# Decode attention over a key cache: one early load split by rows into five transfers

## The chip, the cores and the metric

The kernel runs on one core of a Trainium2 chip. The metric is the device time of one execution in microseconds (us). The time before is 1305.89 us, the median of 2 runs (1305.44 to 1306.35).

## The reference

One decode step of a transformer block for a batch of 2: layer norm, attention over a cache of 8192 keys and values for each of 16 heads of 256, then a bilinear feed-forward block. All is float32. The key and value caches are 268 MB each, so nearly all of the work is to read them once.

```python
B, Sq, D = 2, 1, 448
H, Sk, Dh = 16, 8192, 256
...
q = (layernorm(x) @ wq).reshape(B, Sq, H, Dh).transpose(0, 2, 1, 3)
scores = einsum("bhqd,bhkd->bhqk", q, k_cache) * (Dh ** -0.5)
p = softmax(scores, axis=-1)
o = einsum("bhqk,bhkd->bhqd", p, v_cache)
h = x + o.transpose(0, 2, 1, 3).reshape(B, Sq, H * Dh) @ wo
...
g, u = layernorm(h) @ w_gate, layernorm(h) @ w_up
h2 = h + (g * u) @ w_down
```

## The kernel before

A "query" is one pair of head and batch item; there are NQ = 32. Query i has 8192 keys, laid out so that each of the 128 partitions holds NJ = 64 keys in a row: `keys(cache, i, lo, hi)` is the view of keys lo to hi of every partition, 1 KB per key and partition. A load of all 64 keys is 8.4 MB in 128 rows of 64 KB; a load of 16 keys is 2.1 MB in 128 rows of 16 KB.

The keys go to `k_sb`, which has room for 112 keys per partition: query 0, 2, 4 ... sit at keys 0 to 63 (`k_base` 0), query 1, 3, 5 ... at 48 to 111. The 16 places in the middle are shared, so the keys of query n+1 can be loaded once the first part of query n (its HC = 16 keys in the shared places) has been scored. The values go to `v_sb`, one buffer of 64, reloaded when TensorE has used it up. The weights of the next heads go to `w_sb`.

All these loads are issued by SP, in the order of the program, on one queue. An order waits on SP until its buffer is free, and the loads behind it wait with it. The order is: the weights of the first heads (`d_w0`), query 0's keys in three pieces (`FIRST`: keys 48 to 64, 0 to 16, 16 to 48), query 1's keys, query 0's values, query 2's keys, weights, query 1's values, and so on. The last queries' values are cut into smaller pieces (`LATE`), and the weights of the feed-forward block come last, into `k_sb`. ACT's queue has only the load of x at the start and half of the output at the end.

VectorE does the scores: a product of the keys with the query, written over the keys (`tensor_mul`), and a sum over the 256 entries (`tensor_reduce`). `score_parts` cuts a query in two parts (16 and 48 keys), and for the queries in `FINE` (0, 30 and 31) in four of 16. For query 0 these are keys 48 to 64, 0 to 16, 16 to 32 and 32 to 48. TensorE and ScalarE do the softmax's sums and exponentials and the mix of the values.

Waits are worked out by the class `Orders`. Each order names the regions that it reads and writes; a load writes a region of `k` given in elements of a partition's row, and gets a semaphore of its own name, which counts to 16. An order that touches a region waits for every load whose region overlaps it. A region of `k` says nothing of partitions.

Every instruction but the DMA issues is recorded by one helper, so the profile shows line 206 for nearly all of them and line 154 for the DMA issues; they are told apart by their tiles.

Of the kernel before, what the change touches and what calls it, by code (L numbers as in the profile page):

```python
# [10 lines left out]
B, D, H, SK, DH, F = 2, 448, 16, 8192, 256, 1792  # L11
EPS = 1e-5
P = 128
# [38 lines left out]
EARLY = NQ - len(LATE)  # L52
LOOP = EARLY
DOWN = (4, 4, 4, 2)
FINE = (0, NQ - 2, NQ - 1)


# [136 lines left out]
def decode_block(nc, x, k_cache, v_cache, w, wg, wu, wd, out):  # L194
    o = Orders(nc)

    def sb(name, *shape):
        return nc.alloc_sbuf_tensor(name, list(shape), F32)[:]
# [25 lines left out]
    k_sb = sb("k_sb", P, 2 * NJ - OVER, DH)  # L224
# [4 lines left out]
    def keys(cache, i, lo, hi):  # L229
        h, b = divmod(i, B)  # L230
        return cache[b, h].rearrange("(p j) d -> p j d", p=P)[:, lo:hi, :]

    def load_keys(name, cache, i, lo, hi, buf, at, event=None):
        o.load(
            "SP", name, buffers[buf][:, at : at + hi - lo, :], keys(cache, i, lo, hi),
            writes=[(buf, at * DH, (at + hi - lo) * DH)], event=event,
        )

    def k_base(i):
        return i % 2 * (NJ - OVER)  # L240

    def load_k(i, lo=0, hi=NJ):
        load_keys(f"d_k_{i}_{lo}", k_cache, i, lo, hi, "k", k_base(i) + lo)
# [15 lines left out]

    load_w("d_w0", 0, 0, WQ)  # L260
    for lo, hi in FIRST:
        load_k(0, lo, hi)

    ident = sb("ident", P, P)
    put("POOL", "memset", ident, 0.0, w=["ident"])
# [82 lines left out]
    for k in range(2):  # L348
        for b in range(B):
            for c in range(DC):  # L350
                at = c * 2 * DH + (k * DH if c < DC - 1 else 0)
# [47 lines left out]
    def score_parts(i):  # L399
        at = [(k - 1) % (NJ // HC) * HC if i % 2 == 0 else k * HC for k in range(NJ // HC)]  # L400
        if i in FINE:
            return [(lo, lo + HC) for lo in at]
# [141 lines left out]
    for n in range(NQ + 1):  # L544
        hp, at = divmod(n, 2 * B)
# [53 lines left out]
    for name, t, src in (("wg", wg_t, wg), ("wu", wu_t, wu)):  # L599
        for k, half in enumerate(halves):  # L600
            o.load("SP", f"d_{name}_{k}", t[:, half], src[:, half],
                   writes=[("k", places[name] + half.start, places[name] + half.stop)])
    at = 0
    for n in DOWN:
        o.load("SP", f"d_wd_{at}", wd_t[:, at * D : (at + n) * D], wd[:, at * D : (at + n) * D],
               writes=[("k", at * D, (at + n) * D)])
# [181 lines left out]
```

## Time and profile before

| what | value |
|---|---|
| time, median of 2 runs | 1305.89 us (1305.44 to 1306.35) |
| profiled execution, its own time | 1305.48 us |
| its span | 1304.1 us |
| VectorE busy | 1130.9 us (87%) |
| TensorE matmul busy | 489.5 us (38%) |
| ScalarE busy | 62.7 us (5%) |
| read from memory | 561.19 MB, 430 GB/s over the span |

The span is the time from the first to the last instruction that the profiler saw; the profiled execution took 1.4 us more than that. The page's slices give the busy share in tenths of each engine in 40 equal pieces of the span; the row DMA is the mean over the core's 16 DMA engines. The chain that ended last is followed back from the last instruction, at each step to what released it. In an issue row the last number is the median time from the issue to the landing. A packet in the DMA view is a row of a transfer, or a completion of 4 bytes, which counts one of a semaphore's 16 steps.

### The profile page before, as it was taken

The page shows a single profiled execution, that of the slowest core. Times are in us where ns is not written, and L with a number is a line of the kernel's source. Part 1 is how long each engine was busy: PE and PEld are TensorE (multiplying, and loading weights), DVE is VectorE, ACT ScalarE, POOL GpSimd, SP SyncE. Part 2 cuts the span into 40 slices and gives each one's busy share as a digit, 9 for nine tenths or more (in the row PEclk, how much of TensorE's full clock was granted, in tenths as well). Part 3 has the DMA queues.
Part 4 walks back from the last instruction along what each step waited for, and adds up shares of the span by engine and source line. Part 5 has one row for each costly group of instructions (what it writes and reads, how often), then busy time and mean ns, then how long its engine had stood idle before and what let it go on. Part 6 is the DMA issues. An engine that isn't in the chain of part 4 may idle for free.

```text
span 1304.1 us, 6966 instructions
## 1 busy us (share of the span) xinstructions
PE 489.5 (38%) x3004; PEld 170.0 (13%) x3004; DVE 1130.9 (87%) x279; ACT 62.7 (5%) x184; POOL 1.3 (0%) x8
## 2 busy tenths in 40 slices
PE   3036332263431634305333243433423334233277
PEld 2012110020100201102101011100101011011013
DVE  7997998878988789987889878889788898899981
ACT  1000000000000000000000000000000000000000
POOL 0000000000000000000000000000000000000000
PEclk8567766686665766658676576665767666566678
DMA  9999999999999999999999999999999999999998
GB/s 413 432 428 447 422 446 422 442 420 446 422 445 416 448 420 448 420 440 438 430 428 440 436 424 444 424 421 441 446 422 442 418 446 422 445 425 427 432 423 363
DMA packets 13136, 561.35 MB, mean 430 GB/s; under 512 B 1474, under 2 KB 1476, under 8 KB 2372
## 3 DMA queue, kind: packets, MB, share of 16 engines
q1 hardware_dynamic: 13112, 561.19, 99.7%
q8 instruction: 7, 0.11, 0.0%
q14 instruction: 5, 0.04, 0.0%
q10 hardware_dynamic: 12, 0.01, 0.0%
HBM read 561.19 MB, written 0.00 MB: 430 GB/s over the span
## 4 chain that ended last, share of the span: by engine, by line
DMA 73%; DVE 25%; PE 1%; issue 0%; ACT 0%; SPq 0%; POOL 0%; POOLq 0%; DVEq 0%
DMA k_sb<-in_A_k_cache_dram 68%; DVE k_sb L206 12%; DVE s L206 12%; DMA k_sb<-in_A_v_cache_dram 3%; DMA k_sb<-in_wd_dram 3%; DVE nm L206 0%; PE o_ps L206 0%; PE q_ps L206 0%; PE sm L206 0%; PE y_ps L206 0%; DVE xb L206 0%; DVE o_ps L206 0%; SPq L154 0%; ACT o_sb L206 0%; POOL ident L206 0%
## 5 line engine op out<-in xcount | busy, mean ns | idle before, releaser
L206 DVE TENSOR_TENSOR k_sb<-k_sb,q 128x4096 f32<-128x4096 f32 x70 | 556.4, 7949 | 133.6 <-DMA k_sb<-in_A_k_cache_dram 129.9
L206 DVE TENSOR_REDUCE s<-k_sb 128x16 f32<-128x4096 f32 x70 | 556.1, 7945 | 0.3
L206 PE MATMUL o_ps<-v_sb,p 128*2 128x512 f32 x2000 | 292.2, 746 | 397.5 <-PEq L161 374.6
L206 PEld LDWEIGHTS o_ps<-v_sb,p 128*2 128x2 f32 x2000 | 54.2, 97 | 606.8 <-issue 579.6
L206 PE MATMUL sm<-nm,row 1*128 1x1 f32 x64 | 16.8, 329 | 195.9 <-PEq L161 172.4
L206 PE MATMUL sm<-ident,m 128*1 128x128 f32 x32 | 10.6, 331 | 140.9 <-PEq L161 101.0
L206 PE MATMUL q_ps<-w_sb,xb 128*128 128x256 f32 (+1 forms) x172 | 59.2, 502 | 0.0
L206 ACT ACTIVATE o_sb<-o_ps 128x512 f32<-128x512 f32 x32 | 19.1, 597 | 689.2 <-PE o_ps L206 689.2
L206 PE MATMUL sm<-sel,o_sb 128*128 128x1 f32 x256 | 33.7, 253 | 25.7 <-PEq L161 22.1
L206 PEld LDWEIGHTS sm<-nm,row 1*128 1x128 f32 x64 | 14.8, 287 | 205.2 <-issue 180.3
L206 PE MATMUL acc_ps<-w_sb,oT 128*2 128x448 f32 x60 | 36.3, 743 | 12.4 <-PEq L161 11.6
L206 PEld LDWEIGHTS sm<-sel,o_sb 128*128 128x128 f32 x256 | 31.8, 195 | 56.1 <-issue 46.5
L206 PEld LDWEIGHTS q_ps<-w_sb,xb 128*128 128x128 f32 x172 | 33.6, 200 | 30.0 <-issue 27.6
L206 PE MATMUL sm<-lsum,ones 128*128 128x1 f32 x64 | 17.3, 339 | 26.0 <-PEq L161 22.3
L206 ACT ACTIVATE nb<-sm 128x1 f32<-128x1 f32 x32 | 5.5, 171 | 414.9 <-PE sm L206 414.9
L206 PEld LDWEIGHTS sm<-ident,m 128*1 128x1 f32 x32 | 2.6, 80 | 152.3 <-issue 109.3
L206 PEld LDWEIGHTS sm<-lsum,ones 128*128 128x128 f32 x64 | 15.4, 298 | 28.0 <-issue 23.9
L206 ACT ACTIVATE q<-q_ps,rstd 128x512 f32<-128x512 f32 (+1 forms) x18 | 11.5, 640 | 70.6 <-PE q_ps L206 70.6
L206 DVE TENSOR_REDUCE total<-o_ps 128x1 f32<-128x128 f32 x1 | 0.3, 292 | 15.7 <-PE o_ps L206 15.7
L206 ACT ACTIVATE p<-s,nb 128x64 f32<-128x64 f32 x32 | 11.2, 349 | 1.0
L206 PE MATMUL q_ps<-k_sb,xr 128*32 128x256 f32 (+1 forms) x128 | 10.3, 445 | 0.7 <-DVE xr L206 0.7
L206 ACT ACTIVATE oT<-sm,rl 128x2 f32<-128x2 f32 x32 | 8.4, 262 | 39.1 <-PE sm L206 39.1
(80 smaller groups left out, 78.3 us busy)
## 6 DMA issues: line engine op xcount, KB each, us to landing
v_sb<-in_A_v_cache_dram SPq DMA_DIRECT2D x4, 4096.0 KB, 30.6
w_sb<-in_w_dram SPq DMA_DIRECT2D x7, 1792.0 KB, 33.6
v_sb<-in_A_v_cache_dram SPq DMA_DIRECT2D x1, 7168.0 KB, 26.3
v_sb<-in_A_v_cache_dram SPq DMA_DIRECT2D x1, 6144.0 KB, 28.4
k_sb<-in_A_k_cache_dram SPq DMA_DIRECT2D x2, 2048.0 KB, 11.2
k_sb<-in_A_k_cache_dram SPq DMA_DIRECT2D x1, 4096.0 KB, 24.2
k_sb<-in_A_v_cache_dram SPq DMA_DIRECT2D x1, 4096.0 KB, 37.7
v_sb<-in_A_v_cache_dram SPq DMA_DIRECT2D x3, 1024.0 KB, 23.4
```

The lines of the kernel that those rows point to most:

```text
L206: o.put(engine, lambda: f(*args, **kw), r, w, mark, event)
```

## The change

The second of query 0's three loads, keys 0 to 16 of all 128 partitions, becomes five loads of the same keys: partitions 0 to 111, 112 to 119, 120 to 123, 124 and 125, and 126 and 127. They are issued by SP one after the other at the place of the old load, each with a semaphore of its own. Their regions are cut so that they don't overlap each other: each names a few elements of the row and the last the rest of it. VectorE's product on keys 0 to 16 of query 0 reads all of that region, and so waits for the five semaphores instead of one. Nothing else differs in the order of any engine's instructions.

```diff
 DOWN = (4, 4, 4, 2)
+ROWS = (112, 8, 4, 2, 2)
...
     load_w("d_w0", 0, 0, WQ)
     for lo, hi in FIRST:
-        load_k(0, lo, hi)
+        if lo > 0:
+            load_k(0, lo, hi)
+            continue
+        at = 0
+        for n in ROWS:
+            o.load(
+                "SP", f"d_k_0_{lo}_{at}", k_sb[at : at + n, lo:hi, :],
+                keys(k_cache, 0, lo, hi)[at : at + n], writes=[("k", lo * DH + at, lo * DH + (at + n if at + n < P else hi * DH))],
+            )
+            at += n
```

## The prediction

> **What bounds the kernel now.** I read first the page's totals and its slices, then the chain that ended last in order of time, then SP's own timeline.
>
> ```profile
> span 1304.1 us, 6966 instructions
> ...
> DMA  9999999999999999999999999999999999999998
> ...
> q1 hardware_dynamic: 13112, 561.19, 99.7%
> ...
> q10 hardware_dynamic: 12, 0.01, 0.0%
> HBM read 561.19 MB, written 0.00 MB: 430 GB/s over the span
> ```
>
> SP's queue q1 fills 99.7% of the time of all 16 DMA engines, in every slice but the last. The kernel moves 561 MB and does little else that costs time. The chain says how the other engines fit in:
>
> ```profile
> 51.73 4.34 DVE s L206
> 56.08 28.28 DMA k_sb<-in_A_k_cache_dram
> 84.39 4.42 DVE k_sb L206
> 88.81 0.19 DVE nm L206
> 89.00 4.34 DVE s L206
> 93.36 34.00 DMA k_sb<-in_A_k_cache_dram
> ...
> 1265.47 34.42 DMA k_sb<-in_wd_dram
> 1299.90 0.14 issue
> ```
>
> VectorE appears with 9 us per query between a landing of keys and the issue of the next keys. That does not make it a bound. The DMA engines hold other work in those 9 us, which SP's timeline shows (issue times, first column):
>
> ```profile
> 1.19 19.76 SPq L154 DMA_DIRECT2D k_sb<-in_A_k_cache_dram  x4
> 20.99 0.43 SPq L154 DMA_DIRECT2D v_sb<-in_A_v_cache_dram  x1
> 56.08 0.33 SPq L154 DMA_DIRECT2D k_sb<-in_A_k_cache_dram  x1
> 74.31 0.33 SPq L154 DMA_DIRECT2D v_sb<-in_A_v_cache_dram  x1
> 93.36 0.33 SPq L154 DMA_DIRECT2D k_sb<-in_A_k_cache_dram  x1
> 117.98 0.33 SPq L154 DMA_DIRECT2D v_sb<-in_A_v_cache_dram  x1
> ```
>
> The values issued at 74.31 are queued when the keys land at 84.39. They are 8.4 MB, 19 us of work, and the next keys are issued 9 us later, at 93.36. In the next round the values come at 117.98 and the keys land at 127.36 (93.36 + 34.00). So each engine's own queue always has work in it, and the end is set by the engine that finishes its bytes last. The windows view gives the rate of the middle (second to last number the share of the engines, last GB/s):
>
> ```profile
> 200.00:1200.00 1000.00, 359.27 (x2078) 119.91 (x2082) 883.03 (x180) 44.87 (x138) 0.00 (x0) 0.65 1.00 433
> ```
>
> 433 GB/s over 16 engines is 27.1 GB/s each. One row of the changed load (16 keys of 256 floats, 16,384 B) therefore costs its engine 0.605 us.
>
> **The change part by part.** The bytes stay the same. What changes is which engine moves which row, four more issues on SP, and four more semaphores in one wait of VectorE.
>
> *Engines used.* The trace tells how short transfers are spread. Two of them go through ACT's queue, x (2 rows) and half of the output (4 rows):
>
> ```profile
> x_sb<-in_A_x_dram ACTq DMA_DIRECT2D x1, 3.5 KB
> out_dram<-y ACTq DMA_DIRECT2D x1, 1.8 KB
> ```
>
> Queue q10 counted 12 packets: 2 rows and 2 completions, 4 rows and 4 completions. So a transfer of n rows, for n of 2 or 4, used n engines, a row each. The old load gave 8 rows to each of 16 engines. In the new form 112 rows give 7 each, and the remaining 16 rows go out as 8, 4, 2 and 2 over at most as many engines. Two bounds follow. If the four leftovers took 16 different engines, every engine has 8 rows as before: 0 us. If each transfer starts its count at the same engine, two engines have 7 + 1 + 1 + 1 + 1 = 11 rows, two have 9, four have 8 and eight have 7. The two are then late by 3 x 0.605 = 1.8 us, and eight are ahead by 0.6 us. No row tells which engine a transfer starts at; I take the stacked end, as nothing in the trace suggests that a transfer continues where the last one stopped. [...]
>
> *Does being late once cost anything at the end?* All engines run at one speed and none runs dry, so a late engine has no chance to catch up. The kernel already shows this. Around 22 us an instruction fetch of 16 KB is among the packets (DMA view of 20 to 30 us, first row). Of the 16 completions of query 2's keys 15 fall between 81.5 and 82.9 us (second row) and the last between 83.5 and 84.5 (third):
>
> ```profile
> q8 instruction: 1, 0.02, 0.6%
> ...
> DMA packets 44, 0.42 MB, mean 297 GB/s; under 512 B 15, under 2 KB 15, under 8 KB 15
> ...
> DMA packets 33, 0.46 MB, mean 459 GB/s; under 512 B 1, under 2 KB 1, under 8 KB 1
> ```
>
> One engine is at least 0.6 us behind all others sixty microseconds after that fetch, and VectorE starts at 84.39, with that last one. So what counts is the lateness of the last engine. If a stacked engine is late already, its 1.8 us come on top in full; if it is one of the early ones, part of the 1.8 us hides behind the present straggler. If the straggler is one of the eight that lose a row, the end could even come 0.6 us earlier. The bounds of this part are -0.6 and +1.8; I take +1.8, since with two engines stacked, one that is already behind is enough, and other fetches can still make one so.
>
> *The start, where the change sits.* The three loads of query 0's keys, as the view of that tile in the first 15 us has them, then the issues of 20 to 30 us with their time to landing:
>
> ```profile
> L154 SPq DMA_DIRECT2D k_sb<-in_A_k_cache_dram x3: 412/432/703, 1.2 to 2.1; - x3
> DMA to landing us min/median/max: 9.0/13.4/24.2
> ...
> k_sb<-in_A_k_cache_dram SPq DMA_DIRECT2D x1, 25.0
> v_sb<-in_A_v_cache_dram SPq DMA_DIRECT2D x1, 44.0
> ```
>
> Keys 48 to 64 land at 10.2, keys 0 to 16 (the changed ones) at about 15.0, keys 16 to 48 at 26.3, query 1's keys at about 45.6, query 0's values at 65.0. VectorE needs them here:
>
> ```profile
> 11.72 4.42 DVE L206 TENSOR_TENSOR k_sb<-k_sb,q 128x4096 f32<-128x4096 f32 x1 [3.67 <-ACT q L206]
> ...
> 20.51 4.42 DVE L206 TENSOR_TENSOR k_sb<-k_sb,q 128x4096 f32<-128x4096 f32 x1
> ...
> 29.30 4.42 DVE L206 TENSOR_TENSOR k_sb<-k_sb,q 128x4096 f32<-128x4096 f32 x1
> ...
> 47.12 4.42 DVE L206 TENSOR_TENSOR k_sb<-k_sb,q 128x4096 f32<-128x4096 f32 x1
> ```
>
> The changed keys have 5.5 us to spare, the next ones 3.0, query 1's 1.5. A lateness of 1.8 us is thus covered by VectorE's own first products, but for 0.3 us at 47.12. Those move the issue at 56.08, and there query 0's values (until 65.0) still fill the engines: 8.9 us of cover. Nothing of the start reaches the end but the lateness of the engines themselves, once.
>
> *Four more issues on SP.* 4 x 0.43 to 4 x 0.70, 1.7 to 2.8 us. Behind them on SP stands the load of keys 16 to 48, issued at 2.1 now and at 3.8 to 4.9 then. The engines are busy with earlier rows until about 15.0, so it costs 0. The issue after it, query 1's keys, waits for VectorE until some 20.6 us and doesn't move. Without this cover it would cost its 1.7 to 2.8 us.
>
> *Four more waits on VectorE.* The chain has steps without work between two instructions from the first to the second of these:
>
> ```profile
> 16.15 0.02 issue
> ...
> 47.02 0.10 issue
> ```
>
> At 0.02 to 0.10 us each, 0.1 to 0.4 us ahead of the product at 20.51, under the same 8.9 us of cover: 0.
>
> Sum: 0 + 1.8 + 0 + 0 = +1.8 us. On the profiled span this is 1304.1 + 1.8 = 1305.9 us. The profiled execution took 1305.48, 1.4 us around the span, and the median of the runs is another 0.4 above it: 1305.89 + 1.8 = 1307.7 us.
>
> **The rivals.**
>
> *Spread out, or hidden behind the present straggler.* The four leftovers fall on different engines, or on engines that are early enough. Then the end moves by -0.6 to +0.6 us: 1305.3 to 1306.5. For it speaks the one late engine at 84 us, a good deal of whose lateness a stacked early engine could use. Against it, that two engines of sixteen must both be early.
>
> *Neighbouring rows get in each other's way.* Rows 112 to 127 lie side by side in the on-chip memory, and now several engines write them at the same moment. If four neighbours share one way in, the 8 rows cost 4 turns instead of 1, the 4 rows 4, the pairs 2 each: 7 + 12 = 19 rows' time on the stacked engines against 8, or 11 x 0.605 = 6.7 us. If the 16 rows go wholly one after the other, 7 + 16 - 8 = 15 rows, 9.1 us. That gives 1312.6 to 1315.0; it decides once two engines slow each other at all. The one place where the trace has it is x, whose two rows go to partitions 0 and 1 (DMA view of 1.55 to 1.90 us, GB/s by slices of 8.75 ns, and its queue):
>
> ```profile
> GB/s 0 0 0 0 0 0 0 0 0 0 0 0 0 205 0 0 205 0 0 0 0 0 0 0 0 1638 819 0 1638 0 819 0 0 0 819 0 819 0 1638 0
> ...
> q10 hardware_dynamic: 4, 0.00, 2.9%
> ```
>
> The two rows start 26 ns apart. All four packets together took 2.9% of 16 x 350 ns, 162 ns, so at most 81 ns a row, where 1,792 B at 27.1 GB/s are 66 ns: they overlap and pay little. But 1.8 KB say little on 16 KB. [...]
>
> *Slower by far: engines out of step lose rate.* If the engines, once out of step by up to 2.4 us (11 rows against 7), disturbed each other in the 1000 us of the middle, 2% of the rate (433 down to 424 GB/s) would cost 26 us: 1332 or more. It decides from that rate on. Against it: one engine is out of step from 22 us on already, and the rate of the middle is 433.
>
> **How the numbers follow.** The stacked engines, paid once (+0.6 to +2.2 us): 0.45. Spread or hidden (-0.6 to +0.6): 0.25. Neighbours in the way (+2.2 to +9.2): 0.24. Lost rate, or another way beyond 26 us: 0.04. Another way ahead by over 26 us: 0.01, as 1304.1 us of span with 99.7% busy engines leave no such room. The last hundredth lies between. The range goes from -0.7 to +9.2 us, 1305.2 to 1315.1, and holds the first three but for some of their edges. A change of 2%, 26 us, is about what a measurement of this kernel can tell from none: slower by more 0.04, faster by more 0.01, within 0.95.
>
> **What would show it.** Right: keys 0 to 16 land by about 17 us in four short transfers and a long one; keys of query 2 land up to 2 us later than 84.36, on two late completions; from there the times run in parallel to the end, and 200 to 1200 us still moves 433 GB/s. Neighbours in the way would show as a landing of the short transfers beyond 20 us, and VectorE waiting before its second product. Lost rate would show as a step from one landing of keys to the next that is longer than 38.7 us, in all rounds alike. The prediction is wrong if the landings are where they were, or the difference to before grows after 100 us.

## The result, and the profile after

The changed kernel takes 1314.95 us (1314.83 to 1315.07) against 1305.89: +9.1 us, ratio 1.0069 with a 95% interval of 1.0053 to 1.0086. That is slower, though by far less than 2%. The profiled execution took 1314.83 us with a span of 1313.4, 9.3 us more than before.

The page of the changed kernel first: the same bytes, a little less of the engines' time, and 16 packets more on q1 (13128 against 13112), the further completions of the short loads.

```profile
span 1313.4 us, 6972 instructions
...
q1 hardware_dynamic: 13128, 561.19, 99.5%
```

Where the time goes is seen in the windows view of both kernels, over the 20 us around the changed load. The last two columns are the share of the engines' time that packets took (it can pass 1, as a packet counts where it starts), and GB/s. Before:

```profile
10.00:15.00 5.00, 5.00 (x21) 4.27 (x21) 3.28 (x1) 1.17 (x3) 0.00 (x0) 1.00 1.08 465
15.00:20.00 5.00, 2.38 (x9) 1.06 (x7) 4.96 (x2) 0.73 (x2) 0.00 (x0) 1.00 0.97 419
20.00:25.00 5.00, 0.00 (x0) 0.00 (x0) 4.97 (x3) 0.00 (x0) 0.00 (x0) 0.65 1.21 514
```

and after, with the middle of the kernel as its last row:

```profile
10.00:15.00 5.00, 5.00 (x21) 4.30 (x20) 3.06 (x1) 0.95 (x2) 0.00 (x0) 1.00 0.99 282
15.00:20.00 5.00, 2.60 (x10) 1.25 (x8) 4.96 (x2) 0.95 (x2) 0.00 (x0) 1.00 1.17 174
20.00:25.00 5.00, 0.00 (x0) 0.00 (x0) 0.82 (x1) 0.00 (x0) 0.00 (x0) 0.67 0.83 262
...
200.00:1200.00 1000.00, 369.19 (x2117) 120.67 (x2109) 884.40 (x176) 45.06 (x137) 0.00 (x0) 0.65 1.00 433
```

The engines stay nearly as busy (0.83 to 1.17) and move half as much. In these 15 us they are behind by (183 + 245 + 252) x 5 us, 3.4 MB, which at 433 GB/s is 7.9 us. A little of that comes back in the next windows: over the first 100 us the mean is 398 GB/s against 426, 2.8 MB or 6.5 us. That is the mean of 16 engines; the landings below go by the last one. The middle has its old rate. The chain of the changed kernel shows that the loss is carried to the end unchanged (the helper's line is 207 here and the DMA issues' 155, as the kernel is one line longer above them):

```profile
63.35 29.64 DMA k_sb<-in_A_k_cache_dram
93.02 4.42 DVE k_sb L207
101.98 34.01 DMA k_sb<-in_A_k_cache_dram
...
1278.01 30.42 DMA k_sb<-in_wd_dram
1308.43 0.14 issue
1308.56 2.46 PE y_ps L207 x48
```

Query 2's keys land at 92.99 instead of 84.36 (+8.6), the next at 135.99 instead of 127.36 (+8.6), the last weights at 1308.43 instead of 1299.90 (+8.5). The rest of the 9.3 is in the tail: the last matmuls take 2.46 us on the chain instead of 1.57.

VectorE does wait at the start, but that is not what costs. Its timeline after:

```profile
25.66 4.42 DVE L207 TENSOR_TENSOR k_sb<-k_sb,q 128x4096 f32<-128x4096 f32 x1 [4.84 <-DMA k_sb<-in_A_k_cache_dram]
...
34.96 4.42 DVE L207 TENSOR_TENSOR k_sb<-k_sb,q 128x4096 f32<-128x4096 f32 x1 [0.42 <-DMA k_sb<-in_A_k_cache_dram]
...
54.38 4.43 DVE L207 TENSOR_TENSOR k_sb<-k_sb,q 128x4096 f32<-128x4096 f32 x1 [1.51 <-DMA k_sb<-in_A_k_cache_dram]
```

Its 6.8 us of waits, and a start 0.2 us later, make up nearly all of the 7.3 us by which the issue of query 2's keys moves, from 56.08 to 63.35. Query 0's values, issued at 21.24, land 52.4 us later, at 73.6, and fill the engines until then, so the issue still comes 10 us early.

### The profile page after: what moved, and what is told of

Its sections match the earlier page's. It is cut to its first block, busy times and chain, and to the rows that moved or that the text cites. A ratio compares the mean times of both kernels' runs of the same rounds, so it can differ in the third digit from the quotient of the medians.

```text
span 1313.4 us, 6972 instructions
## 1 busy us (share of the span) xinstructions
PE 495.4 (38%) x3004; PEld 171.2 (13%) x3004; DVE 1131.2 (86%) x279; ACT 62.6 (5%) x184; POOL 1.3 (0%) x8
## 3 DMA queue, kind: packets, MB, share of 16 engines
q1 hardware_dynamic: 13128, 561.19, 99.5%
## 4 chain that ended last, share of the span: by engine, by line
DMA 73%; DVE 26%; PE 1%; SPq 0%; issue 0%; ACT 0%; DVEq 0%
DMA k_sb<-in_A_k_cache_dram 70%; DVE k_sb L207 13%; DVE s L207 13%; DMA k_sb<-in_wd_dram 2%; DVE nm L207 0%; SPq L155 0%; PE q_ps L207 0%; PE y_ps L207 0%; DMA x_sb<-in_A_x_dram 0%; PE sm L207 0%; DVE xb L207 0%; ACT q L207 0%; DVE m L207 0%; DVE sum_sq_x L207 0%; DVE sum_x L207 0%
## 5 line engine op out<-in xcount | busy, mean ns | idle before, releaser
L207 PE MATMUL sm<-ident,m 128*1 128x128 f32 x32 | 10.5, 329 | 142.1 <-PEq L162 103.1
L207 PE MATMUL acc_ps<-w_sb,oT 128*2 128x448 f32 x60 | 36.5, 749 | 12.4 <-PEq L162 11.7
L207 PE MATMUL o_ps<-k_sb,p 128*2 128x512 f32 x48 | 9.6, 956 | 6.1 <-DMA k_sb<-in_A_v_cache_dram 6.1
## 6 DMA issues: line engine op xcount, KB each, us to landing
v_sb<-in_A_v_cache_dram SPq DMA_DIRECT2D x1, 7168.0 KB, 27.1
```

What stands on the lines that cost most here:

```text
L207: o.put(engine, lambda: f(*args, **kw), r, w, mark, event)
```

## The experiments

Each changes only how keys 0 to 16 of query 0 (or, where said, another early load) are fetched. Times are medians against the kernel before, run on the same chip. The edits are against the kernel before unless said otherwise. Beside the views, the trace keeps the time of every single row; some of these are named below. In the kernel before, every 16 KB row of the changed load took 0.61 us, the 32 KB rows of the load behind it 1.21 (one, just after an instruction fetch, 1.71).

**1. Two loads, 112 and 16 rows.** Counted as 7 rows and 1 row on each of 16 engines, none has more than 8.

```diff
-        load_k(0, lo, hi)
+        if lo > 0:
+            load_k(0, lo, hi)
+            continue
+        rows = [(s, s) for s in (slice(0, 112), slice(112, P))]
+        for at, (dst, src) in enumerate(rows):
+            o.load(
+                "SP", f"d_k_0_{lo}_{at}", k_sb[dst, lo:hi, :], keys(k_cache, 0, lo, hi)[src],
+                writes=[("k", lo * DH + at, lo * DH + at + 1 if at + 1 < len(rows) else hi * DH)],
+            )
```

> Two loads in place of the five: 112 rows, then 16 rows. With packets of one row the 16 rows can take 16 engines, so every engine moves 7 + 1 = 8 rows as before. Three theories. Neighbours: rows of neighbouring partitions that several engines write at once hold each other up; the load of 112 rows took 8.1 us in the changed kernel instead of 4.3 (7 rows at 0.61), and the 16 rows would take 4 turns instead of 1, another 1.8 us: +4 to +6 us. Stacking: only the number of rows on the fullest engine counts: 0 us. Count: every further transfer costs the same, 9.1 us for four of them: +2.3 us.

Measured: 1310.42 against 1305.76 us, +4.7 us, ratio 1.0038 (1.0023 to 1.0052). Stacking alone is out: half of the loss is there with 8 rows on every engine by that count (the queue counts 16 completions for each of the two loads). The count of loads (+2.3) is too small: the interval is 3.0 to 6.8 us. The load of 112 rows is slow by itself: half of its rows took 1.0 us or longer, where all took 0.61 before.

**2. Five loads cut by keys.**

```diff
-        load_k(0, lo, hi)
+        if lo > 0:
+            load_k(0, lo, hi)
+            continue
+        for a, b in ((0, 4), (4, 8), (8, 12), (12, 14), (14, 16)):
+            load_k(0, a, b)
```

> Five loads in the same place, but cut by keys (4, 4, 4, 2 and 2 keys of all 128 partitions) instead of by partitions. Neighbours: every engine writes the partitions that it writes in all other loads: 0 us. Stacking: 8 rows on every engine in each load: 0 us. Count: four further transfers as in the change: +9.1 us.

Measured: 1306.01 against 1305.76, +0.25 us, ratio 1.0003 (0.9993 to 1.0013). Four further loads, issues and waits cost nothing that can be measured (the interval is -0.9 to +1.7 us) when each load covers all 128 partitions.

**3. Two loads of 64 rows.** As experiment 1 but for one line:

```diff
+        rows = [(s, s) for s in (slice(0, 64), slice(64, P))]
```

> Two loads of 64 rows each. 16 engines with 4 rows each, twice: 8 rows as before. Neighbours: 16 engines now write into half of the partitions at a time; if the ways into them are as many as the engines that a full load uses, each row takes twice as long, 8 x 0.61: +4.9 us. Stacking: 0 us. Count: +2.3 us.

Measured: 1311.46 against 1305.76, +5.7 us, ratio 1.0044 (1.0027 to 1.0061). Counted as 4 rows of each load on each of 16 engines, the work is spread evenly, and it still takes about twice its 4.9 us. The middle one of its rows took 1.26 us, twice 0.61, and the windows view of this kernel shows about half the rate:

```profile
10.00:15.00 5.00, 5.00 (x18) 4.12 (x18) 3.29 (x1) 0.95 (x2) 0.00 (x0) 1.00 1.00 213
15.00:20.00 5.00, 3.09 (x13) 1.68 (x11) 4.97 (x2) 0.95 (x2) 0.00 (x0) 1.00 1.11 256
```

**4. Sixteen loads of 8 rows, four partitions apart.** Again one line differs from experiment 1:

```diff
+        rows = [(s, s) for s in (slice(32 * g + j, 32 * g + j + 29, 4) for g in range(4) for j in range(4))]
```

> Sixteen loads of 8 rows, each of 8 partitions that lie four apart (0, 4, ... 28, then 1, 5, ... and so on), so that no two rows of a load come from one group of four. Neighbours: nobody is held up, but eight engines move 16 rows each and eight none: 8 x 0.61, +4.9 us, by stacking alone. Stacking: the same +4.9 us. Count: fifteen further transfers at 2.3 us, +34 us.

Measured: 1314.85 against 1305.76, +9.1 us, ratio 1.0068 (1.0051 to 1.0084). Count is out (+34). But +9.1 is more than the 4.9 that both other theories gave. The DMA view has the reason. The loads' completions (packets under 512 B, eight to a load) from 10.5 to 15.1 us and from 15.1 to 24.5 us:

```profile
DMA packets 126, 1.18 MB, mean 256 GB/s; under 512 B 60, under 2 KB 60, under 8 KB 60
...
DMA packets 154, 2.21 MB, mean 235 GB/s; under 512 B 60, under 2 KB 60, under 8 KB 60
```

Sixty completions, seven and a half loads, in 4.6 us: 0.61 us a load, the price of a free row. Then sixty in 9.4 us: 1.25 us a load, twice that. The first half are the loads to partitions 0 to 63. In the second half the short rows go to partitions 64 to 127, and the reading, which no run shows by itself, is that rows of the load behind go there at the same time from the other eight engines: those of its 32 KB rows that started from 17 to 20 us took 2.4 to 2.5 us instead of 1.21. The two halves differ in one more thing. The sixteen loads keep SP busy at some 0.6 us each, so the rows of the load behind start only at 14.1 to 15.2 us, and in the first half the other eight engines have nothing to do. Experiment 11 tells the two apart: there such short rows go to partitions 0 to 31 beside the rows of the load behind, and all keep their 0.61 and 1.21 us. The second half by itself was not tried.

**5 to 8. Neighbours or apart, on which side?** 112 rows as in the change, and the other 16 as four loads of 4 rows; near is four neighbouring rows, apart is four rows at a step of four. The line for near on chip (the first list) and near in memory (the second):

```diff
+        rows = [(slice(0, 112),) * 2, *zip([slice(112 + 4 * j, 116 + 4 * j) for j in range(4)], [slice(112 + 4 * j, 116 + 4 * j) for j in range(4)])]
```

Apart is `[slice(112 + j, 125 + j, 4) for j in range(4)]`. The kernels have (near, near), (apart, apart), (near, apart) and (apart, near).

> 112 rows as in the change, then four loads of 4 rows, each of four neighbouring partitions. All four fall on the same four engines: 7 + 4 = 11 rows, as many as in the change. Stacking alone: 3 rows more than 8, +1.8 us, and some 3 to 4 us for the slow load of 112 rows (it landed 3.7 us late in the kernel with 112 and 16 rows): +5 us. Neighbours: the four rows of a load take turns, 16 turns and 7 rows against 8, 15 x 0.61 = 9.2 us, and part of the slow 112 rows on top: +9 to +12 us.

> The same 112 rows and four loads of 4 rows, but each load takes partitions four apart (112, 116, 120, 124, then 113, 117 and so on), on chip and in memory. Rows, engines and loads are as many as in the kernel with neighbouring rows. Stacking alone: the same time as that one. Neighbours: the rows of a load no longer take turns with each other, only with the load behind them: +5 to +7 us, some 4 to 5 us less than that one.

> As before, but the rows of each small load are neighbours on chip and come from rows four apart in memory, so 16 partitions get another row's keys. Where the cost lies on the chip's side: as with neighbours on both sides, +9 to +12 us. Where it lies on the side of the memory (64 KB between neighbouring rows, 256 KB between these): as with rows apart on both sides, +5 to +7 us.

> The reverse: the rows of each small load lie four partitions apart on chip and are neighbours in memory, so 16 partitions get another row's keys. Chip's side: +5 to +7 us. Memory's side: +9 to +12 us.

| on chip | in memory | us (before 1305.72) | ratio |
|---|---|---|---|
| near | near | 1316.47, +10.8 | 1.0080 (1.0063 to 1.0097) |
| apart | apart | 1312.75, +7.0 | 1.0052 (1.0035 to 1.0069) |
| near | apart | 1317.39, +11.7 | 1.0086 (1.0069 to 1.0103) |
| apart | near | 1312.68, +7.0 | 1.0052 (1.0035 to 1.0069) |

The time follows the place on chip; where the rows come from makes no difference that shows. The four kernels have as many loads of as many rows, so stacking cannot tell them apart, and neighbours do. The rows' own times say it most directly: near on chip, twelve of the sixteen short rows took 2.4 to 2.5 us, four times 0.61; apart, none took longer than 1.29. The load of 112 rows took 7.0 to 8.1 us in all four, where seven rows should take 4.2; so some 3 of the 7.0 us that are left with apart are its. The windows view from 15 to 25 us, for (near, near) and then for (apart, apart):

```profile
15.00:20.00 5.00, 3.12 (x13) 1.71 (x11) 4.96 (x2) 0.95 (x2) 0.00 (x0) 1.00 1.23 177
20.00:25.00 5.00, 0.00 (x0) 0.00 (x0) 0.61 (x1) 0.00 (x0) 0.00 (x0) 0.80 0.99 121
```

```profile
15.00:20.00 5.00, 2.98 (x12) 1.60 (x10) 4.96 (x2) 0.95 (x2) 0.00 (x0) 1.00 1.06 236
20.00:25.00 5.00, 0.00 (x0) 0.00 (x0) 3.26 (x2) 0.00 (x0) 0.00 (x0) 0.77 1.02 390
```

**9. Sixteen loads of 8 rows, sixteen partitions apart.** Against experiment 4:

```diff
-        rows = [(s, s) for s in (slice(32 * g + j, 32 * g + j + 29, 4) for g in range(4) for j in range(4))]
+        rows = [(s, s) for s in (slice(j, j + 113, 16) for j in range(16))]
```

> Sixteen loads of 8 rows as in the kernel with rows four apart, but with rows sixteen partitions apart (0, 16, ... 112, then 1, 17 and so on). Groups of four neighbours only: no two rows of a load share a group, as with rows four apart, so the short loads land 0.61 us apart at first and the time is that of the kernel with rows four apart, about +9 us. [...]

Measured: 1327.05 against 1305.90, +21.2 us, ratio 1.0160 (1.0142 to 1.0178). The completions from 11.6 to 15.1 us, and from 11.6 to 37.1 us:

```profile
DMA packets 44, 0.56 MB, mean 159 GB/s; under 512 B 18, under 2 KB 18, under 8 KB 18
...
DMA packets 301, 4.18 MB, mean 164 GB/s; under 512 B 118, under 2 KB 118, under 8 KB 118
```

At eight to a load that is 1.6 us a load at first and 1.7 over all (a few of the later completions may be the load behind's), where rows four apart took 0.61. That is more than the 1.2 of two rows in turn (2 x 0.61). The rows that started from 10.7 to 11.7 us did take 1.2 to 1.3 us; the load behind sets in at 12.7, and from 16 us on most short rows take 1.8, three times 0.61, while its 32 KB rows take 3.0 to 3.6 (three times 1.21 is 3.6). So it isn't distance that keeps rows out of each other's way. "Groups of four neighbours" was too small a rule: no two rows of a load are nearer than 16 here, and they held each other up. Which distance does it this run can't single out, as a load's rows lie 16 to 112 apart; but rows 16 apart (0 and 16) stood together in experiment 4 too, at 0.61.

**10. The change made twice**, on the load of keys 48 to 64 as well (the edit is against the changed kernel).

```diff
-        if lo > 0:
+        if hi - lo > HC:
             load_k(0, lo, hi)
```

> The change made twice: the first of query 0's loads (keys 48 to 64) is split into 112, 8, 4, 2 and 2 rows as well. If an engine that is late stays late to the end and nothing hides it: twice the 9.1 us, +18 us. If the first 9 us go into some slack of the start: much less than +18.

Measured: 1324.57 against 1305.90, +18.7 us, ratio 1.0141 (1.0123 to 1.0159). The cost is paid again in full; there is no slack at the start that takes it.

**11. Six further loads of 8 rows, nothing split.** Stacked, they add six rows to each of eight engines.

```diff
+        if lo == 0:
+            for j in range(6):
+                o.load(
+                    "SP", f"d_more_{j}", v_sb[j % 4 : 29 + j % 4 : 4, j // 4 * HC : (j // 4 + 1) * HC, :],
+                    keys(k_cache, 0, lo, hi)[j % 4 : 29 + j % 4 : 4], writes=[("v", j // 4 * HC * DH + j % 4, j // 4 * HC * DH + j % 4 + 1)],
+                )
```

> Nothing is split. Six further loads of 8 rows (16 keys each, rows four partitions apart) follow the second load, into the still empty buffer of the values: they add six rows to each of eight engines, on the partitions that these engines write anyway. Query 0's values wait for them on SP. Stacking, paid in full: 6 x 0.605, +3.6 us; if the engine that is last now is not one of the eight, its 1.2 to 1.8 us hide a part: +1.8 to +2.4 us. Count: six loads at 2.3 us, +14 us. Nothing is paid for rows on single engines: 0.

Measured: 1309.27 against 1305.90, +3.4 us, ratio 1.0027 (1.0016 to 1.0038). This is stacking by itself: every row kept its 0.61 us. The added 0.79 MB, spread over all engines, would be 1.8 us, below the interval (2.1 to 5.0). The chain shows how it is paid:

```profile
56.56 29.64 DMA k_sb<-in_A_k_cache_dram
95.19 34.87 DMA k_sb<-in_A_k_cache_dram
```

Query 2's keys land at 86.20, 1.8 us later than before; it seems that the straggler of the kernel before is not among the eight and hides a part. Query 3's land at 130.06, 2.7 us later, and the span is 3.5 us longer. The rows were added before 20 us, so the growth comes from something later. Instruction fetches are the candidate: between 50 and 130 us every 64 KB row took 2.42 to 2.44 us but one, at 112.0, which took 3.08, just after a fetch at 111.7. The trace does not name the engine of a packet, so this stays open.

## Why the prediction was right or wrong

The forecast was the stacked engines, +1.8 us, at 0.45; the measured +9.1 lies at the upper end of the rival of neighbouring rows (+6.7 to +9.1), which had 0.24, and 0.15 us inside the range. It came out slower, as forecast, but the mechanism that the forecast put first was not the main one. The step that failed is the price of a row: the sum takes 0.605 us for each, whatever rows are written beside it, and only the rival does not. (The 0.7% was also clear of noise, so the 2% that the prediction held to be the least that can be told from none was too much.)

- *What bounds the kernel:* right. The lateness of early loads goes to the end in full (8.6 us at query 2, 8.5 at the last weights; twice the change, twice the cost).
- *Engines used:* the packets were counted rightly (16 further completions), and that the short loads stack, which the forecast chose without a row to show it, fits the rows of the changed kernel: twice four rows of 16 KB follow one another with at most 3 ns between, one set from 16.45 to 24.46 us and one from 15.72 to 22.56, as if two engines each took a row of all four short loads. These eight rows took 1.25 to 2.39 us each instead of 0.61. But the load of 112 rows was counted as seven rows' time, in the sum and in the rival. In the changed kernel that load landed 17.3 us after its issue, at about 18.9, where the load before it landed at 10.8: 8.1 us where seven rows should take 4.2. The middle one of its rows took 0.9 us instead of 0.61. With 16 rows on 16 engines behind it, +4.7 us in all. This term was left out. Which rows of that load get in each other's way is not known: no run shows which engine moves which of the 112.
- *The neighbours' price:* the turns were about right. That four neighbours share one way in was a supposition of the rival; the runs with 4-row loads then showed rows of four neighbours at 2.4 to 2.5 us, four times 0.61. From 18.9 us to the last landing of the changed keys, at about 25.6, the short loads took 6.7 us, where the rival's 12 turns are 7.3; wholly one after the other would be 9.7. But that the end is +9.1, the rival's upper figure, is in part luck. The changed keys landed 10.6 us later than before (25.6 against 15.0), the slow 112 rows' 3.9 us included, and 2.0 us of that are gone at query 2, where the landing is 8.6 late. That the straggler of the kernel before hides them, as the prediction had it for a stacked engine, fits (its last completion comes 1.2 to 2.0 us after those of the others there, 83.91 against 81.92 to 82.71) and was not tried. The weight given to the rival was too small: x's two rows of 1.8 KB, which overlapped and paid little (at most 81 ns a row in the kernel before), were taken as a sign against. The four kernels with 4-row loads decide for it: near on chip +10.8 and +11.7, apart +7.0 twice.
- *Stacking, once:* exists, at about its price. Six rows were to cost 3.6 us and took 3.4 (2.1 to 5.0), of which only 1.8 showed at query 2.
- *Four issues, four waits:* right, nothing. Cut by keys they cost +0.25 us, inside the interval. The seven first loads of keys were issued by 4.0 us:

```profile
L155 SPq DMA_DIRECT2D k_sb<-in_A_k_cache_dram x7: 253/356/752, 1.2 to 4.0; - x7
DMA to landing us min/median/max: 9.6/17.3/31.0
```

- *Cover at the start:* the changed keys came some 5 us after VectorE wanted them, as the sign of the rival of neighbouring rows had it, and the 8.9 us of cover before query 2's keys were enough all the same: that issue moved by 7.3.
- *Lost rate:* the middle has 433 GB/s, as before, though the last engine is further behind the mean (8.6 us late against 6.5). From 200 to 1200 us all but 5 of some 6200 rows of 64 KB took 2.42 to 2.44 us, and all but 4 before.

## What to carry to other kernels

In this kernel, bound by its loads, what the last DMA engine lost at the start was lost at the end (8.6 us at query 2, 8.5 at the last weights), though the compute engines had 8.9 us of cover. In a kernel bound like it, look for the rate, not for who waits. Load all 128 partitions at once, and cut a transfer by columns if it must be cut (+0.25 us for five loads in place of one). Cut by partitions, even into even halves, the rows took twice as long (the middle one 1.26 us instead of 0.61; +5.7 us for one load of 2 MB), which fits several engines that write through the same way into on-chip memory; that is a reading, as no run names a row's engine. A tiny transfer that seems free in the trace, like x's rows of 1.8 KB (at most 81 ns in the kernel before), need not tell what a large one costs.

## What was not expected of the hardware

- Crowded rows came with slow rows on the other engines too. With four neighbouring rows at a time, four engines move them, a row each, if counted as x's two rows are, which had two completions; yet, in the first of the four kernels with 4-row loads (near, near), from 20 to 25 us the engines' share was 0.99 and they moved 121 GB/s, where the other twelve alone would move 325 at 27.1 GB/s each. The twelve 32 KB rows that the load behind started from 19 to 22 us, beside these short rows, took 4.8 to 5.1 us each instead of 1.21: all twelve were held up alike. What they share with the short rows was not tried.
- Crowded rows took close to whole turns of 0.61 us: about 1.25 with two halves and in the second half of experiment 4, 1.8 in experiment 9, 2.4 to 2.5 with near rows. That these are two, three and four rows on one way is a reading, as no run names a row's engine. The rows of the 112-row loads lie between (the middle one 0.9 to 1.0 us) and stay unexplained.
- The lateness of the landings doesn't shrink. After 100 us those of the changed kernel follow those of before at a nearly fixed distance, for 1200 us (8.6 us late at query 3's keys, 135.99 against 127.36; 8.5 at the last weights, 1308.43 against 1299.90).
